# Six GELU evacuations ahead of the table sines, and two more weight strips on the ScalarE queue

## The chip, the cores and the metric

The kernel runs on one core of a Trainium2 chip. The metric is the device time of one execution in microseconds (us); lower is better. The core has five engines that run side by side: TensorE (PE in the profile, with PEld for its weight loads), VectorE (DVE), ScalarE (ACT), GpSimd (POOL) and SyncE (SP). They meet through semaphores; each takes its instructions in the order of the program. Loads and stores are put on queues by SyncE and ScalarE and carried by 16 DMA engines.

## What is computed

The input x has 2048 rows of 640 numbers in bfloat16. Two branches of it are mixed by a gate for each row:

```python
def _A_ref(x, Lambda_re, Lambda_im, B_re, B_im, C_re, C_im, log_dt, Dskip):
    Lam_bar = jnp.exp(jnp.exp(log_dt) * (Lambda_re + 1j * Lambda_im))
    B_bar = ((Lam_bar - 1.0) / Lam)[:, None] * Bmat
    Bu = jnp.einsum("bld,pd->blp", x + 0j, B_bar)
    for t in range(L):                       # 2048 steps
        h = Lam_bar[None, :] * h + Bu[:, t, :]
    y = 2.0 * jnp.einsum("blp,dp->bld", hseq, Cmat).real + x * Dskip
def _B_ref(x, w1, b1, w2, b2):
    h = _gelu(jnp.einsum("bsd,df->bsf", x, w1) + b1)     # 640 -> 1728, tanh form
    return jnp.einsum("bsf,fd->bsd", h, w2) + b2
g = sigmoid((x * gate_w).sum(-1, keepdims=True))
return g * a + (1 - g) * b
```

Branch A is a complex diagonal recurrence with 640 states, branch B a two-layer network with a GELU between.

## The kernel before

**Tiles and chunks.** The rows are worked in four chunks of 512. For each chunk c, TensorE multiplies by B (`ssm(c)`, matmuls at L536), by the first layer's weights (`ff1(c)`, L253), by the second layer's (`fin_b(c)`, L594 and L610) and by C (`fin_a(c)`, L653). All matmuls write to eight PSUM banks of 128x512 f32, which `bank()` hands out in turn; a bank is written again only after the engine that read it is done.

**First layer.** The 1728 hidden columns are 13 tiles of 128 (kf 0 to 12) and one of 64. The 640 input columns are 5 strips (kd 0 to 4) of weights. `w1a[kd]` holds the first FA = 6 tiles' weights of strip kd, `w1b[kd]` the rest, with one further column in which the gate's weight is put. `ff1_mm` does one matmul; `ff1_act` (L258) takes a full bank out through GELU with the bias `b1_c`, which lies in `colB`.

**The start.** For chunk 0, x is turned by TensorE itself (`turn`, L218, copies at L225 and L227) because it comes first. While the strips arrive, TensorE works kd by kd over six open banks (`strip(kd, ...)`): strips 0 and 2 by quarters of the chunk, then strip 1 whole, then strips 4 and 3 together, bank by bank. Parameters come as short rows in two tiles, `prmA` (log_dt and Lambda) and `prmB` (b1 and gate_w); one matmul with an identity turns each into columns (L329 to `colA`, L391 to `colB`). The matmul of prmB stands between kf 2 and kf 3 of strips 4 and 3. Five copies at L394 then put the gate's column into w1b.

**Tables.** The recurrence is made real by turning each state by its own angle, so cosines and sines of angle times row number are needed for 512 rows. VectorE makes the arguments for 128 rows (`u`, `kk`, `red`, `ab` at L370 to L380, and for a few special angles `two`, `kq`, `redq`, `absq` at L382 to L386). ScalarE takes four sines (L379, L381, L387, L388: `FS`, `FC`, `sq`, `cq`). VectorE extends them to 512 rows (L408 to L422: `TCOS`, `TSIN`). ScalarE computes sine, GELU and exponential from different function tables; a change is an ACT_TABLE_LOAD in the profile.

**The rest of VectorE's work.** For each chunk and each of five groups of states: products with the tables and a scan along the rows (`scan_ops`, L471 and L490). Then it puts x times D into banks (`seed`, L569) ahead of `fin_a`, and mixes the branches (L658). It scales C once (`fold(ks)`, five times): ScalarE makes two scaled copies `ft` (L453, L455; two buffers), VectorE adds them to C (L459). Folds 0 to 2 are put into `fin_b(0)`, folds 3 and 4 into `ff1(2)`, before kf 1 and kf 4. `gates(c)` (L551, L552) makes the gate's two factors from `gz`.

**Order.** Instructions of TensorE, VectorE and ScalarE stay in the order in which the program lists them. A small planner (`ck`, `later`, `let_out`) only chooses, when the program is built, after which group of matmuls a pending VectorE step is listed. The end of the program lists the stages:

```python
    ssm(0); gel_tile(1); ff1(1); gates(0)
    ssm(1, ...); gates(1)
    fin_b(0, {a: (lambda a=a: fold(a)) for a in range(3)})
    ff1(2, 0, {1: fold(3), 4: fold(4), 9: seed(0), 11: seed(1)})
    gates(2); fin_a(0); ssm(2); fin_b(1); fin_a(1); ssm(3); ff1(3)
    fin_b(2); gates(3); fin_a(2); fin_b(3); fin_a(3)
```

(Shortened: lambdas, tile allocations and the loads of x are left out.)

**Loads.** Before, two first strips (w1a 0 and 2) are issued by ScalarE; all other loads are issued by SyncE, in the order in which they stand, x first. There are eight semaphores for the completion of loads, used in turn; a load that reuses one waits on its queue until the earlier load with that semaphore has landed.

Of the kernel before, what the change touches and what calls it, by code (L numbers as in the profile page):

```python
# [11 lines left out]
ACT = mybir.ActivationFunctionType  # L12
# [4 lines left out]
P = 128  # L17
T = 2048
D = 640
F = 1728  # L20
CH = 512
NCH = T // CH
KD = D // P
# [12 lines left out]
TWO_PI_M = float(np.float32(2.0 * np.pi * (1.0 - 2.0 ** -20)))  # L36
# [5 lines left out]
def kernel(  # L42
# [19 lines left out]
    nc = tc.nc  # L62
# [12 lines left out]
    def bank(dtype=F32):  # L75
        return ps.tile([P, CH * 4 // (4 if dtype == F32 else 2)], dtype, name="bank")


    cut1 = FA * P
    n1b = F - cut1 + 1  # L80
    xT = [const.tile([P, KD, CH], BF16, name=f"xT{c}") for c in range(NCH)]
    w1a = [const.tile([P, cut1], BF16, name=f"w1a_{kd}") for kd in range(KD)]
    w1b = [const.tile([P, n1b], BF16, name=f"w1b_{kd}") for kd in range(KD)]
# [6 lines left out]
    ident = const.tile([P, P], BF16, name="ident")  # L90
    prmA = const.tile([P, P], BF16, name="prmA")
    NB = KS + KF - 1
    prmB = const.tile([P, P], BF16, name="prmB")
    colA = const.tile([P, 3 * KS], F32, name="colA")
    colB = const.tile([P, NB], F32, name="colB")
# [10 lines left out]
    halfpi = const.tile([P, 1], F32, name="halfpi")  # L106
# [8 lines left out]
    def load_xn(c, a0=0, a1=TPC, queue=None):  # L115
        if a0 == 0:
            xn[c] = xnp.tile([P, TPC, D], BF16, name="xn")
        r0 = c * CH + a0 * P
        (queue or nc.sync).dma_start(out=xn[c][:, a0:a1, :], in_=x2d[r0:r0 + (a1 - a0) * P, :].rearrange("(a p) d -> p a d", p=P))

    def load_w1a(queue, kd):
        queue.dma_start(out=w1a[kd][:], in_=B_w1[kd * P:(kd + 1) * P, 0:cut1])

    def rows(queue, dst, v):
        queue.dma_start(out=dst, in_=v.rearrange("(j p) -> j p", p=P))  # L125
# [2 lines left out]
    load_w1a(nc.scalar, 0)  # L128
    load_xn(0, 1, 2)
    load_w1a(nc.scalar, 2)  # L130
    warm = const.tile([P, 1], F32, name="warm")
    nc.scalar.activation(out=warm[:], in_=nc.const_aps.tensor(1.0, [P, 1], BF16), func=ACT.Exp)
    load_xn(0, 2, 3)
# [3 lines left out]
    rows(nc.sync, prmA[0:KS, :], A_log_dt)  # L137
    rows(nc.sync, prmA[KS:2 * KS, :], A_Lambda_im)
    rows(nc.sync, prmA[2 * KS:3 * KS, :], A_Lambda_re)
    for kd in (1, 4, 3):  # L140
        load_w1a(nc.sync, kd)
    rows(nc.sync, prmB[KS:NB, :], B_b1[0:(KF - 1) * P])
    rows(nc.sync, prmB[0:KS, :], gate_w)
    for kd in range(KD):
        nc.sync.dma_start(out=w1b[kd][:, 0:F - cut1], in_=B_w1[kd * P:(kd + 1) * P, cut1:F])  # L145
    make_identity(nc, ident[:])
    HC = CH // 4
    tfi = work.tile([P, HC], I32, name="e")
# [55 lines left out]
    def act(cost):  # L204
        ck.act = max(ck.act, ck.pe + 0.2) + cost
        return ck.act
# [6 lines left out]
    pA = bank()  # L213
# [25 lines left out]
    def col(name, dtype=F32, n=KS):  # L239
        return const.tile([P, n], dtype, name=name)  # L240
# [10 lines left out]
    def ff1_mm(p, c, kf, kd, t0=0, t1=CH, first=None, last=KD - 1):  # L251
        w = w1a[kd][:, kf * P:(kf + 1) * P] if kf < FA else w1b[kd][:, (kf - FA) * P:(kf - FA + 1) * P]
        nc.tensor.matmul(p[:, t0:t1], lhsT=w, rhs=xT[c][:, kd, t0:t1],  # L253
                         start=(kd == 0) if first is None else first, stop=(kd == last), skip_group_check=first is not None)
        pe(t1 - t0)

    def ff1_act(p, c, kf):
        nc.scalar.activation(out=gel[c][:, kf, :], in_=p[:, :], func=ACT.Gelu_apprx_tanh, bias=b1_c[:, kf:kf + 1])  # L258
        act(0.69)
# [51 lines left out]
    def strip(kd, t0, t1, first, f0=0, f1=FA):  # L311
        for kf in range(f0, f1):
            ff1_mm(banks[kf], 0, kf, kd, t0, t1, first, 3)
# [29 lines left out]
    strip(0, HT + P, CH, True)  # L343
    strip(2, HT + P, CH, False)
    strip(1, 0, CH, False)


    HB = 2 * HC

    def scratch(i):  # L350
        return scr[:, i * KS * HC:(i + 1) * KS * HC].rearrange("p (k i) -> p k i", k=KS)

    u, red, ab = scratch(0), scratch(1), scratch(2)
    m1, m2 = scratch(3), scratch(4)
    FSC = hsp.tile([P, 2 * KS, HB], F32, name="hs")
    FS = FSC[:, 0:KS, :]
    FC = FSC[:, KS:2 * KS, :]
# [3 lines left out]
    redq = col("redq", n=NQ * KS)  # L361
    absq = col("absq", n=NQ * KS)
    sq = col("sq", n=NQ * KS)
    cq = col("cq", n=NQ * KS)
# [11 lines left out]
    sQ, cQ = sq[:, 3 * KS:4 * KS], cq[:, 3 * KS:4 * KS]  # L376


    nc.scalar.activation(out=FS[:, :, 0:HC], in_=red, func=ACT.Sin, scale=TWO_PI_M)  # L379
    nc.vector.scalar_tensor_tensor(out=ab, in0=red, scalar=-1.0, in1=red, op0=ALU.mult, op1=ALU.max)  # L380
    nc.scalar.activation(out=FC[:, :, 0:HC], in_=ab, func=ACT.Sin, scale=-TWO_PI_M, bias=halfpi[:])  # L381
    nc.vector.tensor_tensor(out=two[:].rearrange("p (n k) -> p n k", n=NQ), in0=thp_c[:].rearrange("p (o k) -> p o k", o=1).to_broadcast([P, NQ, KS]),  # L382
                            in1=span4[:].rearrange("p (n o) -> p n o", o=1).to_broadcast([P, NQ, KS]), op=ALU.mult)
    nc.vector.tensor_copy(out=kq[:], in_=two[:])
    nc.vector.tensor_tensor(out=redq[:], in0=two[:], in1=kq[:], op=ALU.subtract)
    nc.vector.scalar_tensor_tensor(out=absq[:], in0=redq[:], scalar=-1.0, in1=redq[:], op0=ALU.mult, op1=ALU.max)  # L386
    nc.scalar.activation(out=sq[:], in_=redq[:], func=ACT.Sin, scale=TWO_PI_M)  # L387
    nc.scalar.activation(out=cq[:], in_=absq[:], func=ACT.Sin, scale=-TWO_PI_M, bias=halfpi[:])  # L388
    for kf in range(FA):
        if kf == 3:  # L390
            nc.tensor.matmul(pA[:, 0:NB], lhsT=prmB[:], rhs=ident[:, 0:NB], start=True, stop=True, skip_group_check=True)  # L391
            nc.vector.tensor_copy(out=colB[:], in_=pA[:, 0:NB])
            for j in range(KD):
                nc.vector.tensor_copy(out=w1b[j][:, n1b - 1:n1b], in_=pA[:, j:j + 1])  # L394
        for kd in (4, 3):
            ff1_mm(banks[kf], 0, kf, kd, 0, CH, False, 3)
    for kf in range(FA):
        ff1_act(banks[kf], 0, kf)
    two_banks = [bank(), bank()]
    for kd in range(KD):  # L400
        for i in range(2):
# [327 lines left out]
```

## Time and profile before

| what | us |
|---|---|
| three runs, device time | 216.41, 372.45, 215.88 (median 216.41) |
| the profiled execution, device time | 216.61 |
| its span in the profile | 214.7 |
| TensorE busy (matmuls) | 209.7 |
| VectorE busy | 190.2 |
| ScalarE busy | 101.4 |

The span runs from the first to the last instruction of the program; 1.9 us of the device time lie around it. A line of the timeline gives start, duration, engine, source line, operation, output<-inputs, shape and count, and in brackets the idle time before it with what ended it. A line of the waits gives who waited for whom, the total, the number of times and the longest. Names with q (SPq, ACTq) are the engines' sequencers, which issue loads.

### The profile page before, as it was taken

Reading aid. Unit: us, or ns where it says so; the run is one execution under the profiler, and the core shown is the slowest. Engines: PE = TensorE matmul, PEld = TensorE weight load, DVE = VectorE, ACT = ScalarE, POOL = GpSimd, SP = SyncE. Lnnn points to the kernel's source line nnn. Section 1 sums busy time; section 2 is a strip of 40 time slices with the busy share of each in tenths; the row PEclk is TensorE's granted clock in tenths of the full one; section 3 lists DMA queues with packets and bytes.
Section 4 is the critical chain, followed back from the end, with each engine's and each line's share of the span. In section 5 each row is a group of like instructions: output and inputs, shape, how many; then the busy total and the mean of one; then the engine's idle time right before and its main releaser. Section 6 shows DMA issues by size and latency. Waiting matters only on the chain.

```text
span 214.7 us, 3536 instructions
## 1 busy us (share of the span) xinstructions
PE 209.7 (98%) x1366; PEld 117.1 (55%) x1385; DVE 190.2 (89%) x396; ACT 101.4 (47%) x183; POOL 1.1 (0%) x12
## 2 busy tenths in 40 slices
PE   8999999999999999999999999999999999999994
PEld 4745444454455644775445577444454567654774
DVE  2899999999999999899999999999999999983153
ACT  3599556665875696302572310356683423204200
POOL 1000000000000000000000000000000000000000
PEclk9999999999999999999999999999999999999999
DMA  6899999993000000051000005100000000100011
GB/s 201 251 177 232 219 220 374 170 225 92 3 0 0 3 2 0 12 183 64 0 0 3 0 0 186 61 2 0 0 3 14 0 3 31 61 31 3 0 66 61
DMA packets 30419, 15.84 MB, mean 74 GB/s; under 512 B 22978, under 2 KB 30402, under 8 KB 30402
## 3 DMA queue, kind: packets, MB, share of 16 engines
q1 hardware_dynamic: 29970, 15.18, 29.3%
q10 hardware_dynamic: 432, 0.43, 0.6%
q8 instruction: 11, 0.18, 0.3%
q14 instruction: 6, 0.05, 0.1%
HBM read 7.48 MB, written 2.62 MB: 47 GB/s over the span
## 4 chain that ended last, share of the span: by engine, by line
PE 93%; DMA 3%; SPq 1%; issue 1%; DVE 0%
PE bank L594 26%; PE bank L253 23%; PE bank L653 20%; PE bank L536 20%; DMA w1b<-in_B_w_dram 3%; PE bank L215 1%; PE bank L610 1%; PE bank L279 1%; SPq L145 1%; PE bank L218 0%; SPq L125 0%; DVE ot L658 0%; DVE xT L225 0%; PE bank L269 0%
## 5 line engine op out<-in xcount | busy, mean ns | idle before, releaser
L594 PE MATMUL bank<-w_sb,gel 128*128 128x128 bf16 (+1 forms) x408 | 56.9, 297 | 0.7 <-issue 0.5
L594 PEld LDWEIGHTS <-gel 128*128 128x128 bf16 x416 | 32.2, 98 | 25.5
L539 ACT ACTIVATE bu<-bank 128x512 bf16<-128x512 f32 x40 | 23.9, 597 | 39.4 <-PE bank L536 39.3
L258 ACT ACTIVATE gel<-bank,colB 128x512 bf16<-128x512 f32 x52 | 34.1, 694 | 11.9 <-PE bank L253 11.1
L653 PEld LDWEIGHTS <-hs 128*128 128x128 bf16 x330 | 31.6, 98 | 11.5
L490 DVE TENSOR_TENSOR_SCAN g<-r_c,carry,v 128x512 bf16<-128x512 f32 x30 | 37.4, 1272 | 0.0
L602 ACT ACTIVATE gb<-bank,gcol 128x512 f32<-128x512 f32 (+1 forms) x32 | 15.1, 527 | 35.4 <-PE bank L610 19.3
L253 PE MATMUL bank<-xT,w1b 128*128 128x512 bf16 x137 | 31.0, 379 | 0.4 <-DMA w1b<-in_B_w_dram 0.2
L253 PE MATMUL bank<-xT,w1a 128*128 128x512 bf16 (+1 forms) x152 | 27.7, 334 | 0.2
L653 PE MATMUL bank<-CT_re,hs 128*128 128x320 bf16 (+2 forms) x165 | 27.1, 295 | 0.0
L653 PE MATMUL bank<-CT_im,hs 128*128 128x320 bf16 (+2 forms) x165 | 27.1, 295 | 0.0
L658 DVE SCALAR_TENSOR_TENSOR ot<-bank,gcol,gb 128x320 bf16<-128x320 f32 (+2 forms) x33 | 17.6, 535 | 9.2 <-PE bank L653 8.7
L536 PE MATMUL bank<-xT,BT_im 128*128 128x512 bf16 x99 | 24.8, 379 | 0.1
L536 PE MATMUL bank<-xT,BT_re 128*128 128x512 bf16 x97 | 24.4, 379 | 0.2
L253 PEld LDWEIGHTS <-w1b 128*128 128x128 bf16 x140 | 13.6, 98 | 16.9 <-DMA w1b<-in_B_w_dram 0.7
L253 PEld LDWEIGHTS <-w1a 128*128 128x128 bf16 x156 | 13.8, 101 | 12.5
L569 DVE TENSOR_TENSOR bank<-xn,Dbc 128x320 f32<-128x320 bf16 (+2 forms) x33 | 14.5, 483 | 3.5 <-ACT gb L602 3.4
L536 PEld LDWEIGHTS <-BT_im 128*128 128x128 bf16 x100 | 9.8, 98 | 11.8
L471 DVE TENSOR_TENSOR v<-wa,wb 128x512 bf16<-128x512 bf16 x40 | 15.2, 421 | 0.6
L536 PEld LDWEIGHTS <-BT_re 128*128 128x128 bf16 x100 | 9.6, 98 | 11.0
L583 ACT ACTIVATE bank<-b2bc 128x512 f32<-128x512 bf16 (+1 forms) x24 | 11.7, 529 | 6.2 <-DVE ot L658 6.2
L471 DVE TENSOR_TENSOR wa<-TCOS,g 128x1024 bf16<-128x1024 bf16 x20 | 13.7, 687 | 0.1
(100 smaller groups left out, 151.5 us busy)
## 6 DMA issues: line engine op xcount, KB each, us to landing
out_dram<-ot SPq DMA_DIRECT2D x15, 160.0 KB, 1.8
xn<-in_A_x_dram SPq DMA_DIRECT2D x6, 320.0 KB, 3.2
w_sb<-in_B_w_dram SPq DMA_DIRECT2D x3, 480.0 KB, 4.0
w1b<-in_B_w_dram SPq DMA_DIRECT2D x5, 240.0 KB, 6.1
xn<-in_A_x_dram SPq DMA_DIRECT2D x4, 160.0 KB, 3.1
w_sb<-in_B_w_dram SPq DMA_DIRECT2D x1, 640.0 KB
w1a<-in_B_w_dram SPq DMA_DIRECT2D x3, 192.0 KB, 2.9
w1a<-in_B_w_dram ACTq DMA_DIRECT2D x2, 192.0 KB, 3.6
```

Source lines behind the costliest of these rows:

```text
L253: nc.tensor.matmul(p[:, t0:t1], lhsT=w, rhs=xT[c][:, kd, t0:t1], start=(kd == 0) if first is None else first, stop=(kd == last), skip_grou ...
L258: nc.scalar.activation(out=gel[c][:, kf, :], in_=p[:, :], func=ACT.Gelu_apprx_tanh, bias=b1_c[:, kf:kf + 1])
L471: nc.vector.tensor_tensor(out=o, in0=a, in1=b, op=op)
L490: nc.vector.tensor_tensor_scan(s["g"][:, ri, :], r_c[:, ks:ks + 1].to_broadcast([P, CH]), s["v"][:, ri, :], init, ALU.mult, ALU.add)
L536: nc.tensor.matmul(p[:], lhsT=BT[ks >= KSA][:, kd, (ks % KSA if ks < KSA else ks - KSA) * P:][:, 0:P], rhs=xT[c][:, kd, :], start=(kd == 0 ...
L539: nc.scalar.activation(out=bu[:, ri, :], in_=p[:], func=ACT.Identity)
L569: dve_now(ck.pe, 0.45, lambda: nc.vector.tensor_tensor(out=p[:, 0:d1 - d0], in0=xn[c][:, a, d0:d1], in1=Dbc[:, d0:d1], op=ALU.mult))
L583: nc.scalar.activation(out=v, in_=src, func=ACT.Identity)
L594: nc.tensor.matmul(p[:, col:col + d1 - d0], lhsT=gel[c][:, kf, a * P:(a + 1) * P], rhs=w2_sb[:, kf, d0:d1], start=False, stop=False, skip_ ...
L602: nc.scalar.activation(out=gbs[ti][:, d0:d1], in_=p[:, col:col + d1 - d0], func=ACT.Identity, scale=gcol[:, 1, ti:ti + 1])
L653: nc.tensor.matmul(p[:, 0:d1 - d0], lhsT=hs[c][:, j, lo:lo + P], rhs=CT[:, j % KS, d0:d1], start=False, stop=(j == 2 * KS - 1), skip_group ...
L658: nc.vector.scalar_tensor_tensor(out=ot[:, d0:d1], in0=p[:, 0:d1 - d0], scalar=gcol[:, 0, ti:ti + 1], in1=gbs[ti][:, d0:d1], op0=ALU.mult, ...
```

## The change

Four things move; all other work is the same.

- The strips w1a 1 and w1a 4 are issued by ScalarE, after 0 and 2 and ahead of its warm-up activation. SyncE keeps only w1a 3.
- On SyncE the first part of w1b follows w1a 3, ahead of prmB's rows; the other four parts come after these.
- The matmul of prmB, the copy to colB and the five copies of the gate's column stand right behind strip 1 in the program, ahead of the table's arguments on VectorE and of strips 4 and 3 on TensorE.
- The six GELUs of kf 0 to 5 stand ahead of the four sines on ScalarE.

By the function tables, ScalarE's order is now exponential, GELU, sine, GELU.

```diff
     load_w1a(nc.scalar, 0)
     load_xn(0, 1, 2)
     load_w1a(nc.scalar, 2)
+    load_w1a(nc.scalar, 1)
+    load_w1a(nc.scalar, 4)
     warm = const.tile([P, 1], F32, name="warm")
...
-    for kd in (1, 4, 3):
-        load_w1a(nc.sync, kd)
+    load_w1a(nc.sync, 3)
+    def load_w1b(kd):
+        nc.sync.dma_start(out=w1b[kd][:, 0:F - cut1], in_=B_w1[kd * P:(kd + 1) * P, cut1:F])
+
+    load_w1b(0)
     rows(nc.sync, prmB[KS:NB, :], B_b1[0:(KF - 1) * P])
     rows(nc.sync, prmB[0:KS, :], gate_w)
-    for kd in range(KD):
-        nc.sync.dma_start(out=w1b[kd][:, 0:F - cut1], in_=B_w1[kd * P:(kd + 1) * P, cut1:F])
+    for kd in range(1, KD):
+        load_w1b(kd)
...
     strip(1, 0, CH, False)
+    nc.tensor.matmul(pA[:, 0:NB], lhsT=prmB[:], rhs=ident[:, 0:NB], start=True, stop=True, skip_group_check=True)
+    nc.vector.tensor_copy(out=colB[:], in_=pA[:, 0:NB])
+    for j in range(KD):
+        nc.vector.tensor_copy(out=w1b[j][:, n1b - 1:n1b], in_=pA[:, j:j + 1])
...
-    nc.scalar.activation(out=FS[:, :, 0:HC], in_=red, func=ACT.Sin, scale=TWO_PI_M)
     nc.vector.scalar_tensor_tensor(out=ab, in0=red, scalar=-1.0, in1=red, op0=ALU.mult, op1=ALU.max)
-    nc.scalar.activation(out=FC[:, :, 0:HC], in_=ab, func=ACT.Sin, scale=-TWO_PI_M, bias=halfpi[:])
...
-    nc.scalar.activation(out=sq[:], in_=redq[:], func=ACT.Sin, scale=TWO_PI_M)
-    nc.scalar.activation(out=cq[:], in_=absq[:], func=ACT.Sin, scale=-TWO_PI_M, bias=halfpi[:])
     for kf in range(FA):
-        if kf == 3:
-            nc.tensor.matmul(pA[:, 0:NB], lhsT=prmB[:], rhs=ident[:, 0:NB], start=True, stop=True, skip_group_check=True)
-            nc.vector.tensor_copy(out=colB[:], in_=pA[:, 0:NB])
-            for j in range(KD):
-                nc.vector.tensor_copy(out=w1b[j][:, n1b - 1:n1b], in_=pA[:, j:j + 1])
         for kd in (4, 3):
             ff1_mm(banks[kf], 0, kf, kd, 0, CH, False, 3)
     for kf in range(FA):
         ff1_act(banks[kf], 0, kf)
+    nc.scalar.activation(out=FS[:, :, 0:HC], in_=red, func=ACT.Sin, scale=TWO_PI_M)
+    nc.scalar.activation(out=FC[:, :, 0:HC], in_=ab, func=ACT.Sin, scale=-TWO_PI_M, bias=halfpi[:])
+    nc.scalar.activation(out=sq[:], in_=redq[:], func=ACT.Sin, scale=TWO_PI_M)
+    nc.scalar.activation(out=cq[:], in_=absq[:], func=ACT.Sin, scale=-TWO_PI_M, bias=halfpi[:])
```

## The prediction

> **What bounds the kernel now.** I read the page's busy shares first, then the chain that ended last, then who waited for whom.
>
> ```profile
> PE 209.7 (98%) x1366; PEld 117.1 (55%) x1385; DVE 190.2 (89%) x396; ACT 101.4 (47%) x183; POOL 1.1 (0%) x12
> PE 93%; DMA 3%; SPq 1%; issue 1%; DVE 0%
> PE bank L253 <- DMA w1b<-in_B_w_dram: 0.2, 1, 0.2
> ```
>
> TensorE is busy for 209.7 of 214.7 us and is 93% of the chain. It hardly ever stands still: after the start the waits name one stop, 0.2 us at 15.09, for the last load of w1b (0.39 us, counting the overlap of matmuls that is lost with it). So there is little to gain, and a delay elsewhere costs only if TensorE comes to wait for it. The engine to watch is VectorE, by its waits from 12 to 190 us:
>
> ```profile
> DVE gcol L551 <- ACT gz L285: 0.9, 1, 0.9
> DVE CT_re L459 <- ACT ft L455: 0.7, 2, 0.4
> DVE ot L658 <- DMA out_dram<-ot: 0.3, 1, 0.3
> ```
>
> In 178 us VectorE idles for 1.9 us, in four places. A delay put in at 13 us is thus carried almost whole through the kernel: VectorE has no idle time to make it up. The question is how late it may be before TensorE notices. The stage that the change rebuilds, on ScalarE's timeline:
>
> ```profile
> 8.66 1.28 ACT L379 ACT_TABLE_LOAD   x1
> 10.83 0.74 ACT L379 ACTIVATE hs<-gel 128x640 f32<-128x640 f32 x1 [0.88 <-DVE gel L372]
> 11.69 0.83 ACT L381 ACTIVATE hs<-gel,halfpi 128x640 f32<-128x640 f32 x1
> 12.42 0.20 ACT L387 ACTIVATE sq<-redq 128x20 f32<-128x20 f32 x1
> 12.53 0.30 ACT L388 ACTIVATE cq<-absq,halfpi 128x20 f32<-128x20 f32 x1
> 12.84 1.28 ACT L258 ACT_TABLE_LOAD   x1
> 14.14 7.79 ACT L258 ACTIVATE gel<-bank,colB 128x512 bf16<-128x512 f32 x13
> ```
>
> Columns: start, duration, instruction. The sines end at 12.83, and VectorE's first product with them (L408) starts at 12.86, directly behind its own earlier work. The 13 GELUs run back to back from 14.14, behind TensorE, but TensorE waits for none of them: kf 8's bank is wanted at 15.53 and its GELU has freed it at 14.83, and the later ones have 1.2 us or more.
>
> **What the Trainium skill says.** "ScalarE: Activation LUTs", section "What ACT_TABLE_LOAD costs", prices a change of function set at about 1283 ns of load plus 1380 ns of drain. The trace agrees with the first (1.28 us) and shows no drain: cq ends at 12.83, the load starts at 12.84, the GELU at 14.14. I use 1.30. "Table sets: the hidden batching unit" in the same page advises to batch by set; the change splits the GELUs around the sines, so three loads become four in the program's order. "DMA: Bandwidth & Descriptors", section "Issuing engines are not separate DMA queues", says that loads of ScalarE's and SyncE's queues run on the same 16 DMA engines and interleave. The trace agrees: from 1.75 to 4.3 us both queues moved about 0.39 MB each.
>
> **The change, part by part.**
>
> *Loads.* Two more 192 KB strips are issued on ScalarE's queue by about 2.5 us, beside SyncE's four 160 KB tiles of x. ScalarE's issue time is free: after its warm-up, done at 3.15 before, it waits until 4.44. In the old order the last x tile landed at 5.57 and the prmA rows at 5.80 (semaphore steps in the trace). With even sharing, when SyncE's 640 KB are through, ScalarE's queue has also moved 640 KB instead of 384: 256 KB more, at the page's 251 GB/s, 1.0 us. The last x tile then lands at 6.6, before its use at 7.68. The prmA rows queue behind it and also get new semaphore partners: their third load waits for the second x tile (4.48) instead of the first, so it is issued near 4.5 instead of 3.85. I put prmA at 6.8; TensorE wants it at 6.36. It stops there, so everything behind is x = 0.5 us late. Bounds: 0 (prmA's few rows are not held up) and 1.5 (the tiles of x and prmB, behind w1a 3 and w1b 0 now, come late too). The strips themselves land near 6 to 8, before their use from 9.28 on. w1b 1 to 4 wait for other partners and are issued about half a microsecond later; BT, next on SyncE, had over 4 us to spare (last BT landing 22.64, use 27.05).
>
> *prmB and the GELUs.* The prmB matmul now stands behind strip 1: 10.36 + 0.5 = 10.86. By the prmA pair (matmul 6.36, copy over at 6.76) colB is ready 0.40 later, 11.26. VectorE waits for it before it starts the table's arguments, which were made from 8.59 on under TensorE's strips: 3.79 us of work from u to absq, so done at about 15.5. The GELU needs both a bank and colB, and in the changed program the wait for colB stands ahead of the table load, so the load can't go early: 11.31, first GELU at 12.61. Six GELUs: 0.69 + 5 x 0.58 (four take 2.42) = 3.59, to 16.20; their banks are full by 13.7. Sine table: to 17.50, which hides the arguments' 15.5. First sine to second 0.64, from the second's start to cq's end 1.14 as before: 19.28. VectorE's table products thus start **D = 19.28 - 12.83 = 6.45 us** late. Another GELU table (1.30) follows, then seven GELUs to about 24.8; the first bank that TensorE wants from them is due at 21.65, freed near 21.3, the next ones with growing room. So no early stall there.
>
> *Where D reaches TensorE.* Nothing absorbs D up to the folds of C (L453, L455 on ScalarE, L459 on VectorE), where the two engines wait for each other through two buffers:
>
> ```profile
> 62.97 0.83 ACT L453 ACTIVATE ft<-CT_im,n2im 128x640 f32<-128x640 bf16 x1 [1.21 <-DVE CT_re L459]
> 76.19 0.89 DVE L459 SCALAR_TENSOR_TENSOR CT_re<-CT_re,c2re,ft 128x640 bf16<-128x640 bf16 x1 [0.38 <-ACT ft L455]
> 77.86 0.82 ACT L453 ACTIVATE ft<-CT_im,n2im 128x640 f32<-128x640 bf16 x1
> 78.58 0.82 ACT L455 ACTIVATE ft<-CT_re,n2im 128x640 f32<-128x640 bf16 x1
> 79.30 1.90 ACT L258 ACTIVATE gel<-bank,colB 128x512 bf16<-128x512 f32 x3
> ```
>
> The first line shows ScalarE already waiting for a fold; the later ft had 0.7 to 3.7 us of room, less than D. Behind the last ft (78.58) stand chunk 2's GELUs from kf 4 on. VectorE makes up 0.20 at 70.85 and 0.46 at 76.19, so fold 3 ends at 77.87 + 6.45 - 0.66 = 83.66; the ft behind it starts at 83.70 and ends at 84.52. GELUs of kf 4 to 8, overlapping by 0.10: first end 85.11, fifth 85.11 + 4 x 0.58 = 87.43 instead of 83.35. By the program's buffer order, kf 11's matmuls take the bank that kf 8's GELU frees; they start at 84.62 now and at 87.47 then: **+2.85 us** on TensorE, partly already at kf 10 (83.55, bank of kf 4).
>
> Second place, the seed of chunk 2 that TensorE needs soonest:
>
> ```profile
> 175.83 0.88 DVE L569 TENSOR_TENSOR bank<-xn,Dbc 128x320 f32<-128x320 bf16 x2
> 177.93 0.84 PE L653 MATMUL bank<-CT_re,hs 128*128 128x320 bf16 x5
> ```
>
> The first of these two seeds ends at 176.31, 1.62 before its matmul, and starts right behind a scan, so it shifts with VectorE. By then VectorE has also made up 0.96 at gcol and 0.41 at 97.34: 6.45 - 0.66 - 0.96 - 0.41 = 4.42 late, seed at 180.73, matmul at 177.93 + 2.85 = 180.78. No further stall; but this second place alone would also ask for 2.8. At the end fin_a of chunk 3 has over 4 us of room.
>
> *Sum.* The early 0.5 us and the w1b wait (0.39 back) lie inside the 2.85, because TensorE waits at 84.6 for VectorE's clock and not its own. The end moves by D - 3.60. Against the profiled execution: 216.61 + 2.85 = 219.5. The median shown is 216.41, 0.2 lower, so the forecast is **219.3 us**, 1.3% slower. A comparison of this kernel tells about 2% from no change.
>
> **Rivals.**
> 1. *Not slower*: VectorE's lateness never reaches TensorE, and the loads only fill the w1b gap. This decides if D stays under 3.6. For it: 98% on TensorE, and most waits had over 4 us of room. Against: six GELUs and two table loads alone are 6 us. Time: 216.4 - 0.4 + 0.4 (prmA) = 216.4, or 216.0 with x at 0.
> 2. *The GELU table is loaded at 8.7 after all*, during the wait for colB: D = 5.2, end +1.6, 218.0. Against: the place of the wait in the program's order.
> 3. *Early bandwidth*: the four strips starve x, prmA and prmB. Each microsecond of x adds one to D and so to the end; from x = 2.0 on it passes 2%: D = 7.95, +4.35, 220.8; with x = 2.5, 221.3. For it: the DMA row is full here. Against: only 256 KB are put ahead.
>
> **How the numbers follow.** Forecast 0.65, its own range 218.4 to 220.5 (x from 0 to 1.5, with 0.3 for ScalarE's spacing); rival 1 0.10, rival 2 0.10, rival 3 0.15. The range 217.2 to 221.2 leaves out rival 1 and the far half of rival 3. No case is 2% faster: 0.01. Over 2% slower: rival 3 and the edge of the forecast, 0.16. The rest, 0.83, is within 2%.
>
> **What would show it.** In the profile after: four table loads; first GELU near 12.6, cq's end near 19.3, L408 directly after it with VectorE idle some 4 us before; TensorE waiting for a GELU (L258) at L253 between 83 and 88 us for 2 to 3 us in all; a stop at prmA's matmul of about 0.5. No TensorE wait there, or VectorE idle times of several microseconds between 60 and 100 us that swallow D, would make it wrong; so would prmA or prmB landing over 1.5 us late.

## The result and the profile after

Four executions of the changed kernel took 223.73, 221.37, 224.37 and 221.95 us, median **222.84 us**, against 216.42 for the kernel before on the same chip. The ratio is 1.031 with a 95% interval of 1.020 to 1.041: slower, where 219.3 had been forecast with a range up to 221.2. The profiled execution is the one of 223.73 us, with a span of 221.8 (before 216.61 and 214.7). The granted clock of TensorE, averaged over an execution, was 0.985, 1.0, 0.992 and 0.992 in the four, in this order. It goes with the spread of 3 us only in part: the slowest execution is not the one with the lowest clock. One execution of the kernel before took 372.45 us, for which no trace gives a reason; the ratio leaves it out.

Line numbers are 4 or 5 higher than in the kernel before: L253 is now L258, L258 is L263, L329 is L334, L408 is L412, L453, L455 and L459 are L457, L459 and L463. L391, the matmul of prmB, is L351.

From the page, the busy shares, the chain's shares and the granted clock in 40 slices:

```profile
PE 213.7 (96%) x1385; PEld 118.6 (53%) x1385; DVE 190.3 (86%) x396; ACT 101.4 (46%) x184; POOL 1.1 (0%) x12
PE 61%; DVE 28%; ACT 6%; DMA 3%; issue 1%; SPq 0%; ACTq 0%
PEclk9799999999999999699999999999999999999999
```

TensorE's share of the chain fell from 93 to 61%. VectorE, which had none, has 28%, ScalarE 6%. ScalarE has one instruction more, the fourth table load. TensorE is busy for 4 us more; part of that is 19 more matmuls in the records, and the clock row shows another part: two slices have a lower digit, one at the start and one near 90 us.

The waits, of which four lines carry the reading (who waited for whom, total us, times, longest):

```profile
DVE gel L412 <- ACT cq L402: 4.0, 1, 4.0
DVE colB L352 <- PE bank L351: 2.4, 1, 2.4
PE bank L258 <- ACT gel L263: 2.5, 2, 1.4
PE bank L334 <- DMA prmA<-in_A_Lambda_re_dram: 2.1, 1, 2.1
```

TensorE stops once for the prmA rows, 2.1 us, and twice for a GELU, 2.5 us together. VectorE stands idle for 4.0 us ahead of its first table product. The stop for w1b is gone. The start, from the timeline:

```profile
8.21 0.17 PE L334 MATMUL bank<-ident,prmA 128*128 128x15 bf16 x1 [2.09 <-DMA prmA<-in_A_Lambda_re_dram]
13.35 0.17 PE L351 MATMUL bank<-ident,prmB 128*128 128x18 bf16 x1
13.84 1.28 ACT L263 ACT_TABLE_LOAD   x1 [2.57 <-DVE colB L352]
15.14 3.58 ACT L263 ACTIVATE gel<-bank,colB 128x512 bf16<-128x512 f32 x6
18.73 1.28 ACT L399 ACT_TABLE_LOAD   x1
21.50 0.30 ACT L402 ACTIVATE cq<-absq,halfpi 128x20 f32<-128x20 f32 x1
21.83 0.82 DVE L412 TENSOR_TENSOR gel<-hs,cq 128x640 f32<-128x640 f32 x1 [4.03 <-ACT cq L402]
```

The sines end at 21.80; before it was 12.83. So D, VectorE's lateness, is 8.97 us. And where it reaches TensorE, from the chain in order of time (start, us, what):

```profile
84.55 0.81 DVE CT_re L463
85.38 0.84 ACT ft L457
86.24 0.83 ACT ft L459
87.06 2.90 ACT gel L263 x5
90.00 4.00 PE bank L258 x10
```

A fold on VectorE, two scaled copies on ScalarE, five GELUs, then kf 11's matmuls: the chain that the prediction had drawn, link by link. The matmuls start at 90.00 instead of 84.62, and ten of them take 4.00 us. In the kernel before they stand in a row of 22 without a stop, and these ten took 2.32 us (84.62 to 86.94):

```profile
81.82 5.13 PE L253 MATMUL bank<-xT,w1b 128*128 128x512 bf16 x22
```

For the clock, the busy times in two pairs of stretches of 3.41 us. The columns are the stretch, its length, busy us (and instructions) of PE, PEld, DVE, ACT and POOL, then the granted clock, the DMA share and GB/s:

```profile
4.77:8.18 3.41, 1.36 (x22) 1.12 (x20) 0.62 (x2) 0.54 (x2) 0.00 (x0) 1.00 0.86 281
8.18:11.59 3.41, 3.38 (x33) 3.40 (x34) 1.91 (x9) 1.07 (x4) 0.00 (x0) 0.50 0.75 231
86.69:90.10 3.41, 1.34 (x6) 0.58 (x6) 3.41 (x5) 3.41 (x7) 0.00 (x0) 1.00 0.01 2
90.10:93.51 3.41, 3.41 (x9) 1.22 (x9) 3.41 (x8) 1.98 (x4) 0.00 (x0) 0.50 0.00 0
```

Twice a stretch in which TensorE was busy for only 1.35 us is followed by one at half clock. So each stop was paid twice on the spot: as a wait, and as slow matmuls right after it. What is left of the second payment at the end of the kernel is another matter, taken up below.

### The profile page after: what moved, and what is told of

Same layout as the page of the kernel before. It is cut to its first block, busy times and chain, and to the rows that moved or that the text cites. A ratio compares the mean times of both kernels' runs of the same rounds, so it can differ in the third digit from the quotient of the medians.

```text
span 221.8 us, 3557 instructions
## 1 busy us (share of the span) xinstructions
PE 213.7 (96%) x1385; PEld 118.6 (53%) x1385; DVE 190.3 (86%) x396; ACT 101.4 (46%) x184; POOL 1.1 (0%) x12
## 4 chain that ended last, share of the span: by engine, by line
PE 61%; DVE 28%; ACT 6%; DMA 3%; issue 1%; SPq 0%; ACTq 0%
PE bank L657 20%; PE bank L598 19%; PE bank L258 10%; PE bank L540 10%; DVE g L494 6%; DVE wb L475 4%; DVE wa L475 4%; ACT gel L263 3%; DVE v L475 2%; DVE hs L475 2%; DMA prmA<-in_A_Lambda_re_dram 2%; DVE CT_re L463 1%; DMA w1a<-in_B_w_dram 1%; DVE g L425 1%; DVE TSIN L426 1%; DVE TCOS L426 1%
## 5 line engine op out<-in xcount | busy, mean ns | idle before, releaser
L598 PE MATMUL bank<-w_sb,gel 128*128 128x512 bf16 (+1 forms) x416 | 57.9, 299 | 0.0
L263 ACT ACTIVATE gel<-bank,colB 128x512 bf16<-128x512 f32 x52 | 33.6, 691 | 11.3 <-PE bank L258 11.2
L657 PEld LDWEIGHTS <-hs 128*128 128x128 bf16 x330 | 31.6, 98 | 11.5
L258 PE MATMUL bank<-xT,w1b 128*128 128x512 bf16 x140 | 33.0, 394 | 2.5 <-ACT gel L263 2.5
L258 PE MATMUL bank<-xT,w1a 128*128 128x512 bf16 (+1 forms) x156 | 28.7, 343 | 0.0
L657 PE MATMUL bank<-CT_re,hs 128*128 128x320 bf16 (+2 forms) x165 | 27.1, 295 | 0.0
L657 PE MATMUL bank<-CT_im,hs 128*128 128x320 bf16 (+2 forms) x165 | 27.1, 295 | 0.0
L258 PEld LDWEIGHTS <-w1b 128*128 128x128 bf16 x140 | 14.1, 101 | 20.5 <-issue 5.2
L258 PEld LDWEIGHTS <-w1a 128*128 128x128 bf16 x156 | 14.6, 105 | 12.3
```

What stands on the lines that cost most here:

```text
L598: nc.tensor.matmul(p[:, col:col + d1 - d0], lhsT=gel[c][:, kf, a * P:(a + 1) * P], rhs=w2_sb[:, kf, d0:d1], start=False, stop=False, skip_ ...
L657: nc.tensor.matmul(p[:, 0:d1 - d0], lhsT=hs[c][:, j, lo:lo + P], rhs=CT[:, j % KS, d0:d1], start=False, stop=(j == 2 * KS - 1), skip_group ...
```

## The experiments

The theory to be tested: D reaches TensorE at kf 10 and 11 as D - 3.60; what was missed is a late prmA and the half clock. The rivals: VectorE's lateness costs elsewhere too; the loads alone do it; the four table loads are harmless and only the number of GELUs ahead counts.

| kernel | median us | ratio to before, 95% interval |
|---|---|---|
| the change | 222.84 | 1.0306 (1.0204 to 1.0408) |
| e_order: the new order alone | 220.79 | 1.0233 (1.0199 to 1.0266) |
| e_loads: the new loads alone | 217.30 | 1.0063 (1.0044 to 1.0082) |
| e_order3: three GELUs ahead of the sines | 219.48 | 1.0160 (1.0138 to 1.0182) |
| e_order0: no GELU ahead of the sines | 218.37 | 1.0118 (1.0083 to 1.0153) |
| e_order_xn: e_order, chunk 2's x loaded later | 219.41 | 1.0147 (1.0119 to 1.0175) |
| e_order_ft: e_order, four buffers for ft | 220.37 | 1.0187 (1.0163 to 1.0211) |
| e_after_prmA: the change, prmA's rows early | 223.61 | 1.0355 (1.0321 to 1.0390) |
| e_after_warm: the change, idle TensorE kept busy | 221.15 | 1.0223 (1.0207 to 1.0239) |
| e_loads1: one strip moved instead of two | 216.57 | 1.0034 (1.0017 to 1.0051) |
| e_best: the last part of w1b by ScalarE | 217.86 | 1.0085 (1.0070 to 1.0100) |
| e_best2: the same, later | 218.16 | 1.0111 (1.0069 to 1.0154) |
| e_order_fetch: e_order, TensorE's program made longer ahead | 219.94 | 1.0160 (1.0136 to 1.0184) |

The kernel before lay between 215.95 and 216.42 beside them.

### The two halves apart

**e_order** has the two moves of order with the loads as before (the diff shows part of it):

```diff
     strip(1, 0, CH, False)
+    nc.tensor.matmul(pA[:, 0:NB], lhsT=prmB[:], rhs=ident[:, 0:NB], ...)
+    nc.vector.tensor_copy(out=colB[:], in_=pA[:, 0:NB])
...
     for kf in range(FA):
         ff1_act(banks[kf], 0, kf)
+    nc.scalar.activation(out=FS[:, :, 0:HC], in_=red, func=ACT.Sin, scale=TWO_PI_M)
...
```

> The change without its loads: prmB's matmul behind strip 1 and six GELUs ahead of the sines, all loads as before. Theory (the end moves by D - 3.60, D being how late VectorE's first table product is): no stop at prmA, first GELU near 12.1, cq's end near 18.8, D = 6.0, the matmuls of kf 11 in chunk 2 2.4 us late, 218.8 us; if the two stops before them make TensorE's clock fall to half for the next 3.4 us, up to 220.6. Rival (the loads do all the harm, the new order is hidden): 216.4.

Its sines end at 18.69, D = 5.87: the prediction's own 5.95 (6.45 less its 0.5 for x) within 0.1. kf 11 should then start 2.27 late, at 86.89. TensorE's stops from the timeline (in brackets the idle time and what ended it):

```profile
84.60 1.24 PE L253 MATMUL bank<-xT,w1b 128*128 128x512 bf16 x4 [1.40 <-ACT gel L258]
86.91 2.32 PE L253 MATMUL bank<-xT,w1b 128*128 128x512 bf16 x10 [1.07 <-ACT gel L258]
178.95 0.84 PE L652 MATMUL bank<-CT_re,hs 128*128 128x320 bf16 x5 [1.05 <-DVE bank L568]
182.32 0.84 PE L652 MATMUL bank<-CT_re,hs 128*128 128x320 bf16 x5 [0.50 <-DVE bank L568]
```

kf 11 starts at 86.91, and with no drop of the clock its ten matmuls take 2.32 us again. But two further stops stand at the seeds of chunk 2, the prediction's "second place": the matmul of 177.93 starts at 182.32, 4.39 late, where the prediction's sum gives 2.27. The time is 2.0 us above the expected 218.8, and the clock had no part in it. VectorE did not make up 0.41 us near 97; it lost time there, in a wait of its own:

```profile
102.86 0.55 DVE L657 SCALAR_TENSOR_TENSOR ot<-bank,gcol,gb 128x320 bf16<-128x320 f32 x1 [1.65 <-PE bank L535]
```

The profile names a matmul of ssm as what ended this wait, but that matmul has no part in it. In the profile of the change the same instruction waits 1.34 us and is said to wait for the store, out_dram<-ot. `ot` has two buffers, so L657 waits for the store of two tiles before. I took the store for the cause and tested that in two ways.

**e_order_xn** is e_order with the two loads of x for chunk 2 (320 KB each), which stand on SyncE just ahead of that store, issued by ScalarE after ssm(2):

```diff
     fin_a(0)
-    load_xn(2, 0, H)
-    load_xn(2, H, TPC)
     ssm(2, {KS - 1: lambda: first_banks(1)})
+    load_xn(2, 0, H, nc.scalar)
+    load_xn(2, H, TPC, nc.scalar)
```

> e_order, but the two loads that refill x's tile for chunk 2 are issued by ScalarE after the ssm of chunk 2, and no longer by SyncE between the first two output stores. Theory: in e_order the second store stands behind these 640 KB, and VectorE waits 1.65 us at 102.9 for it, since the output has two buffers; that is what makes it late for the seeds of chunk 2 (TensorE's stops of 1.05 and 0.50 us at 179 and 182). Without the loads in front the wait and both stops go: 219.2, 1.5 less than e_order. Rival (VectorE's lateness comes from the start alone): 220.8 as e_order.

The wait on VectorE and both stops at the seeds are gone, the two at kf 10 and 11 are unchanged (1.41 and 1.07), and the time fell from 220.79 to 219.41. So the wait is for the store, which goes behind the loads of x. In e_order the store was issued at 97.94 and its last part landed at 102.77, 4.8 us later; in the kernel before it took 3.5 us (93.73 to 97.25), and without the loads ahead of it 1.9 us (97.92 to 99.79). In the profiled execution of this kernel (220.31 us; the others took 218.94 to 219.43) the clock dropped once:

```profile
83.08:86.49 3.41, 1.35 (x5) 0.48 (x5) 3.41 (x7) 3.38 (x7) 0.00 (x0) 1.00 0.01 2
86.49:89.90 3.41, 2.94 (x8) 1.01 (x7) 3.41 (x8) 2.47 (x5) 0.00 (x0) 0.50 0.00 0
```

It is the same pattern as in the change, a stretch with 1.35 us busy and then half clock. The same two stops had cost no clock in e_order. Its clock records start at 5.782, and counted from there in steps of 3.413 us the two stops fell into two stretches:

```profile
80.88:84.29 3.41, 2.32 (x11) 0.97 (x10) 3.41 (x6) 1.98 (x3) 0.00 (x0) 1.00 0.00 0
84.29:87.70 3.41, 1.98 (x8) 0.87 (x9) 3.41 (x5) 3.41 (x7) 0.00 (x0) 1.00 0.01 2
```

So the same stops are followed by half clock in one execution and not in another. The drop hides no stop here: the seed was ready at 180.13, and at full clock TensorE would have come for it at about 180.3.

**e_order_fetch** asks why the same store behind the same loads takes longer in e_order than before. In e_order's trace 15 of its 16 parts had landed by 101.69, and the last came 1.1 us later. A fetch of instructions, one packet of 16 KB, was under way at 98.45 for 1.42 us, early in the burst of loads and store; in the kernel before it came at 96.53, at the end of the burst. The guess is that both want the same DMA engine, which the packet records do not name. If the place of the fetch depends on how far a program has been read, a longer program for TensorE ahead of everything should move it, with no change in the work:

```diff
-    for n in (512, 512, 512, 512, 512, 512, 128, 128):
+    for n in (128,) * 26:
         nc.tensor.matmul(pA[:, 0:n], lhsT=ones(P), rhs=ones(n), start=True, stop=True)
```

> e_order with the warm-up of TensorE cut into 26 matmuls of 128 columns instead of 8 of 512 or 128 (3328 columns in both). All work that counts is the same, but TensorE's program is 18 matmuls and as many weight loads longer ahead of everything else. Theory: VectorE's wait for the store of ot near 102.9 us in e_order (1.65 us, against 0.33 in the kernel before) comes from a 16 KB fetch of instructions that shares one DMA engine with the loads of x and the store: the trace shows such a fetch at 98.45 for 1.42 us in e_order, inside the burst from 97 to 102.8, and in the kernel before at 96.53, at the burst's end. With 24 matmuls added to the change, the fetch came 6.5 us earlier against the burst. So here it comes near 93 to 94, ahead of the burst; the wait falls to about 0.3 us, the stops at chunk 2's seeds from 1.55 to at most 0.5, and the time from 220.8 to 219.2 to 219.7 us. Rival: the store is late because it stands behind 640 KB of loads, wherever the fetch falls: wait 1.3 to 1.7, seeds' stops 1.5, 220.8 us.

```profile
101.54 0.55 DVE L657 SCALAR_TENSOR_TENSOR ot<-bank,gcol,gb 128x320 bf16<-128x320 f32 x1 [0.37 <-DMA out_dram<-ot]
```

The fetch came at 95.94 and was over at 97.04, before the burst. All parts of the store landed by 101.45, 3.4 us after its issue at 98.03, and the wait is 0.37 us instead of 1.65: the store behind the loads is not late in itself. The median is 0.85 us lower than that of e_order, less than the 1.1 to 1.6 expected. No stop at the seeds shows, but in the profiled execution the ten matmuls behind kf 11's stop ran at half clock (3.99 us), which made TensorE itself late enough to hide one. An estimate from its times: the seed ended at 180.94 and its matmul started at 181.83; 1.67 us of clock less would have brought TensorE there at 180.16, so about 0.8 us would have been lost, where e_order lost 2.1 (4.39 late there, 2.29 at kf 11). So moving the fetch took away the larger part, not all.

The other profiles line up with this. Counted from the issue of the first load of x, the fetch came after 1.0 to 1.6 us in four kernels (waits 1.51 to 2.11), after 3.2 to 3.3 in two, the change among them (1.34 and 1.25), after 3.7 to 4.0 in five, the kernel before among them (0.33 to 0.61), and ahead of it in two (0.30 and 0.37). That the two share one DMA engine is not shown.

**e_loads** has the loads of the change and the order of before (the diff is the first two parts of the change).

> Only the change's loads: w1a 1 and 4 by ScalarE, w1b 0 ahead of prmB's rows; prmB's matmul and the GELUs where they were. Theory: prmA lands near 8.1, TensorE stops 2.1 us for it and then runs at half its clock to about 11.6 (0.85 us more), gets 0.4 back at w1b: 2.5 us late from its own side. The sines are late by about 2.9, under 3.6, so VectorE adds nothing: 218.9. Rival (early lateness of TensorE is harmless, or the stop comes only with the new order): 216.4.

217.30, less than expected.

```profile
7.29 0.17 PE L334 MATMUL bank<-ident,prmA 128*128 128x15 bf16 x1 [1.13 <-DMA prmA<-in_A_Lambda_re_dram]
```

The prmA rows land at 7.16, the stop is 1.13 us and not 2.1, the clock holds at 1.0, and VectorE's delay (0.93) stays under 3.6, so the stop for prmA is all it costs; w1b's 0.39 us come back. With the order alone at 4.6 us and the loads alone at 1.1, the sum is 5.7 of the 6.4 measured.

### How many GELUs ahead

**e_order3** and **e_order0** are e_order with the first three, or none, of the six GELUs ahead of the sines:

```diff
-    for kf in range(FA):
+    for kf in range(3):
         ff1_act(banks[kf], 0, kf)
     nc.scalar.activation(out=FS[:, :, 0:HC], in_=red, func=ACT.Sin, scale=TWO_PI_M)
...
+    for kf in range(3, FA):
+        ff1_act(banks[kf], 0, kf)
```

> As e_order, but only three GELUs (kf 0 to 2) ahead of the sines, the other three behind them; the same four table loads. Theory: three GELUs less, 3 x 0.58 = 1.74, so D = 4.25 and the end 0.65 later than before: 217.1, with no clock fall. Rival (no threshold, the loss goes with the lateness): two thirds of the loss of e_order or more, so 218.0 or above.

> As e_order, but the four sines ahead of all GELUs again: of the new order only prmB's matmul and the colB copies stay early, and there are three table loads. Theory: VectorE waits for colB before it makes the table's arguments, D = 2.7, under 3.6, so nothing reaches TensorE: 216.4. Rival (every lateness of VectorE is passed on): 219.

D came out at 4.11 (4.25 expected) and 2.54 (2.7 expected), and the stops at kf 10 and 11 are gone in both. The fourth table load is not harmless: in e_order3 the third GELU ends at 13.86 and the first sine starts at 15.17, with nothing but the load of 1.28 us between. Yet both took about 2 us more than expected. In e_order3 the wait for the store of `ot` is 1.79 us and the seeds stop TensorE for 1.36 and 0.50; besides, TensorE stops for banks of the later GELUs, 0.59 us at 18.99 and 0.29 at 19.57. In e_order0 the sines themselves are late, since the copies of prmB now stand ahead of their arguments, and all GELUs behind them:

```profile
17.42 3.40 PE L253 MATMUL bank<-xT,w1b 128*128 128x512 bf16 x15 [1.19 <-ACT gel L258]
```

So ScalarE has two customers at the start, the banks and the tables, and each order of the two makes one of them late. Before, the sines stood first and their arguments were ready at 10.83: both were in time.

### The second buffer of the folds

**e_order_ft** is e_order with four buffers for the scaled copies, in bfloat16, so that ScalarE need not wait for a fold:

```diff
-        t1 = fwork.tile([P, D], F32, name="ft", bufs=2)
-        t2 = fwork.tile([P, D], F32, name="ft", bufs=2)
+        t1 = fwork.tile([P, D], BF16, name="ft", bufs=4)
+        t2 = fwork.tile([P, D], BF16, name="ft", bufs=4)
```

> e_order with four buffers for the scaled copies ft instead of two (in bfloat16, to keep the room), so that ScalarE no longer waits in the folds for VectorE. Theory: the two stops of TensorE at kf 10 and 11 (2.5 us) go, but VectorE is as late as ever, and the stops move to the seeds of fin_a, where TensorE then waits for about 3.5 us in all: 219.9 to 220.8. Rival (the fold is the only place where lateness counts): 218.3.

The stops at kf 10 and 11 are gone, and 2.5 us less of waiting there bought 0.4 us: TensorE now stops at seeds instead, 0.69 us at 88.09, 1.16 at 126.29, 1.17 at 178.89 and 0.50 at 182.26. VectorE's lateness reaches TensorE at the next place where they meet. This is the clearest sign that the lateness, and not a place, is the cause.

### prmA, bandwidth and the clock

**e_after_prmA** is the change with prmA's three row loads issued right behind the first tile of x (the diff shows their new place; they leave the old one).

```diff
     load_w1a(nc.scalar, 0)
+    rows(nc.sync, prmA[0:KS, :], A_log_dt)
+    rows(nc.sync, prmA[KS:2 * KS, :], A_Lambda_im)
+    rows(nc.sync, prmA[2 * KS:3 * KS, :], A_Lambda_re)
     load_xn(0, 1, 2)
```

> The whole change, but with prmA's three rows issued by SyncE right after the first x tile. Theory: no stop at prmA and no clock fall there, so D is 6 again and the end is that of e_order, less the w1b stop of 0.4 where that lies on the path: 220.4 to 220.8. Rival (the strips on ScalarE's queue also hold up x or prmB): 222 and above.

From the waits of SyncE and from the timeline:

```profile
SPq L119 <- DMA w1a<-in_B_w_dram: 1.5, 1, 1.5
6.43 0.45 PE L223 MATMUL bank<-ident,xn 128*128 128x128 bf16 x5 [1.66 <-DMA xn<-in_A_x_dram]
```

The stop at prmA is gone, but the second tile of x lands at 6.38 instead of 4.5 and TensorE stops for it for 1.66 us ahead of 6.43. The three rows take three of the eight semaphores, so SyncE, with the second tile next, waits 1.5 us until a strip has landed, and issues it at 3.69 instead of 1.19. The median is 223.61 where 220.4 to 220.8 was expected: nothing was gained.

**e_after_warm** is the change with 24 matmuls of ones ahead of prmA's matmul, into a corner of the bank that nothing reads, to keep TensorE busy while it waits:

```diff
     strip(0, P, HT, True)
+    for _ in range(24):
+        nc.tensor.matmul(pA[:, CH - 192:CH], lhsT=ones(P), rhs=ones(192), ...)
     nc.tensor.matmul(pA[:, HT:HT + 3 * KS], lhsT=prmA[:], ...)
```

> The whole change, with 24 matmuls of ones (192 columns, 1.9 us, in an unused part of pA) put ahead of prmA's matmul, to keep TensorE busy while it waits. Theory: the stop takes as long as before, but the clock doesn't fall behind it; the strips up to 12 us run at full pace and D is 0.85 smaller where the clock fell before. Median 222, and a narrower spread than the 221.4 to 224.4 of the change. Rival (the slow matmuls at 8 to 11.6 us come from their operands, not from the idle time before): 222.8, with the same slow stretch.

The rows land as late as in the change (8.04 and 8.08), but 1.7 us of the median are back (0.8 had been expected) and all four executions lie within 0.4 us at clock 1.0. From its timeline:

```profile
8.17 0.17 PE L336 MATMUL bank<-ident,prmA 128*128 128x15 bf16 x1 [0.39 <-DMA prmA<-in_A_Lambda_re_dram]
12.17 0.17 PE L353 MATMUL bank<-ident,prmB 128*128 128x18 bf16 x1
```

From prmA's matmul to prmB's it is 4.00 us, as in the kernel before (6.36, and 10.36 for the end of strip 1). In the change it is 5.14 (8.21 to 13.35). So the half clock in the start costs 1.14 us, and useless matmuls are enough to avert it. D is then 7.79, kf 11 starts at 88.83: D - 3.60 = 4.19, measured 4.21. The two stops at kf 10 and 11 are there (1.40 and 1.08) and no drop followed them.

**e_loads1** moves one strip, w1a 1, to ScalarE's queue instead of two, in the order of before.

```diff
     load_w1a(nc.scalar, 2)
+    load_w1a(nc.scalar, 1)
...
-    for kd in (1, 4, 3):
+    for kd in (4, 3):
```

> The kernel before with only w1a 1 moved to ScalarE's queue (192 KB beside x instead of 384). Theory (prmA's rows stand behind x on SyncE's queue and get only half of the engines while ScalarE's queue has strips): prmA lands at about 6.6, between the 5.8 of before and the 7.2 to 8.1 seen with two strips; TensorE stops for 0.3 us or so and has it back at w1b; 216.3, within 0.3 of before. Rival (what matters is which earlier load's semaphore the rows wait for): the third row's load waits for an x tile or strip that lands before 4, as before, so no stop at all.

```profile
6.71 0.17 PE L330 MATMUL bank<-ident,prmA 128*128 128x15 bf16 x1 [0.58 <-DMA prmA<-in_A_Lambda_re_dram]
```

prmA's last row lands at 6.62, against 5.80 with no strip moved and 7.16 with two (e_loads). The first strip of 192 KB delays the rows by 0.82 us, the second by another 0.54. The rival was the semaphore for which the rows' loads wait, and their issue does get later, from 3.85 to 4.18 and 4.82. But the last tile of x, issued at 2.12 each time, lands at 5.57, 6.43 and 7.09, and the rows 0.23, 0.19 and 0.07 us behind it: they come when x is through, so it is the shared transfer that delays them. The median is 216.57, 0.6 above the kernel before at its side, where 0.3 had been expected at most.

In the profile of the change the rows landed at 8.08, with the same loads as e_loads. There four of the five packets of the last row had landed by 7.28 and the fifth came at 8.08, and the other two rows look the same; it was so in e_after_warm too, and not in e_loads. Why one packet lags in one kernel and not in the other was not found.

### The one gain the change has, alone

**e_best** and **e_best2** try to take the 0.39 us of w1b's stop without the rest: the last of w1b's five parts goes to ScalarE's queue, behind its first copy of x (e_best) or behind its last (e_best2).

```diff
-    for kd in range(KD):
+    for kd in range(KD - 1):
         nc.sync.dma_start(out=w1b[kd][:, 0:F - cut1], ...)
...
     nc.scalar.activation(out=r_c[:], in_=dtl[:], func=ACT.Exp)
+    nc.scalar.dma_start(out=w1b[KD - 1][:, 0:F - cut1], ...)
```

> A try for a version faster than both: the kernel before, with the last part of w1b issued by ScalarE behind its copy of the second x tile (near 6.1 us) instead of last on SyncE's queue. Theory: it lands by 12 instead of 15.04, TensorE's stop of 0.39 us goes, nothing else is late since the strips behind it have over 1.4 us of room; VectorE is as late as before and still early enough: 0.4 us less, 0.2%. Rival (it takes bandwidth from w1a 1, prmB or the w1b parts, and the stop comes there): no gain.

> The kernel before with one edit: the last of the five strips of w1b is issued by ScalarE, behind its activation for r_c, that is after its last copy of x, instead of by SyncE. Theory: ScalarE is free there until VectorE delivers the first sine argument, so the issue and its wait for a free queue place hold up nothing that TensorE needs; the strip lands by about 14 us instead of 15.04, the stop of 0.39 us that TensorE makes for it in the kernel before goes, and the time falls by about 0.2 to 0.4 us, to 0.998 to 0.999 of before. Rival: the issue blocks ScalarE past 10.83 us, where its first table load starts in the kernel before; then the sines and GELUs come later by as much, banks are late, and the time is up by 0.5 us or more.

In e_best the part landed at 13.8 and TensorE no longer stopped for it. But ScalarE could not issue the load before 8.63, since its semaphore was still held by a load of prmB, and behind it stood a copy of x:

```profile
9.03 0.21 ACT L332 ACTIVATE dt<-colA 128x5 bf16<-128x5 f32 x1 [3.28 <-DMA prmB<-in_B_b_dram]
9.56 0.27 PE L218 MATMUL bank<-ident,xn 128*128 128x128 bf16 x2 [1.93 <-ACT xT L227]
```

In e_best2 the issue of the load ends at 10.1, about 1.6 us later than that of SyncE's last w1b load in the kernel before (8.53), and the load lands at 16.58 instead of 15.04: TensorE stops 1.39 us for it. Here the theory of a gain and its rival both failed: no GELU became late (D = 0.39) and yet the time rose. No kernel of this study is faster than the one before.

## Why the prediction was wrong, step by step

- **Loads, x = 0.5: the step that failed.** Measured by the matmul of prmB, 13.35 against 10.36, x is 2.99, twice the upper bound of 1.5. With this x alone the forecast would have been 219.3 + 2.5 = 221.8. It has two parts. prmA's matmul is 1.85 late: even sharing put the last tile of x at 6.6 and the rows at 6.8. They landed at 7.09 and 7.16 with the same loads in e_loads, where two strips took 1.36 us and not 1.0, and at 8.08 in the change, where one packet of each row came later still. The further 1.14 us are the half clock after the stop, of which no step took account. That prmA came 2.28 us late was among the prediction's own signs of being wrong. Rival 3 had this mechanism: "each microsecond of x adds one to D and so to the end".
- **prmB and the GELUs: right.** colB to the first GELU, the six GELUs (3.58, forecast 3.59), the table loads (1.28 and nothing behind) and the sines give D = 5.98 + x in the change, against 5.95 + x in the sum. Everything from 11.26 on is late by 2.5, the error of x. Rival 2, the early table load, did not happen: the load at 13.84 waits for colB.
- **Where D reaches TensorE first: right.** kf 11 is 5.38 late, D - 3.60 = 5.37. In e_order it is 2.29 for 2.27, in e_after_warm 4.21 for 4.19, and in e_order_xn, e_after_prmA and e_order_fetch, where D is 5.91, 7.11 and 5.83, it is 2.34, 3.53 and 2.24. The forecast of a wait of 2 to 3 us in all for GELUs held (1.39 and 1.07); it lies from 86.3 to 90.0 rather than between 83 and 88.
- **The clock after these stops: not in the sum.** Ten matmuls took 4.00 us instead of 2.32: 1.68 us. With 1.35 more of the wait at prmA and 1.14 of the first drop, it makes 4.17; on the 219.5 that the prediction gave for the profiled execution, 223.7. It took 223.73. This is an account of that one execution. The others had one drop or none by their mean clock and took 221.37 (none), 221.95 and 224.37 (one each); what else made them differ is in no trace.
- **"VectorE makes up 0.41 at 97.34": wrong, and hidden in the change.** The wait is for a store, which VectorE's own earlier work sets off, so its landing moves along and it is no slack. In e_order it grew to 1.65 us, with an instruction fetch in the burst of its loads and store, and the second place, which the prediction put level with the first, stopped TensorE for another 1.55. In the change the wait was 1.34 us, and no stop shows:

```profile
184.36 0.88 DVE L573 TENSOR_TENSOR bank<-xn,Dbc 128x320 f32<-128x320 bf16 x2
184.99 0.84 PE L657 MATMUL bank<-CT_re,hs 128*128 128x320 bf16 x5
```

  The first of these two seeds ended at 184.83, and its matmul, 7.06 late, started at 184.99. Without the 1.68 us of the second drop TensorE would have come at 183.31 and waited for the seed for about 1.6 us, by an estimate from these times. So the two failures overlap: of the second drop only about 0.1 us is left at the end of the kernel, and a sum with the clock put right would still have missed this place.
- **Rival 1, lateness that never arrives: wrong.** It took D under 3.6 to keep kf 11 in time; e_order0 shows that such an order costs elsewhere.
- **w1b's stop: right**, it is gone and bought nothing.

Part by part, the order alone costs 4.6 us of the 6.4, the loads alone 1.1. The rest, 0.7, appears only with both; a prmB that is late by the loads then delays the GELUs too, and a clock drop at the start stands in no profile but that of the change. It was not split further, and it is smaller than the interval of the change's own ratio (1.020 to 1.041, or 4.4 to 8.8 us), so it may be noise.

## What to carry to other kernels

When an engine with hardly any idle time is made late at the start, look for each place where the bound engine meets it and subtract that place's slack; removing one such place only hands the lateness to the next. Before counting a wait as time to be made up, see whether what ends it is a transfer that moves along. A price read at one place is not yet a price at the end, when a second place would have asked for the same time. A load moved to another queue takes its bandwidth from the loads that the first instructions need, and a load on a compute engine's queue can hold up that engine until a semaphore is free.

## What the runs showed of the hardware

- **A stop of TensorE is followed by half clock, now and then.** The Trainium skill, "TensorE: Matmul & The Clock Gate", section "Part 1: The HAM clock gate (the "warmup" mystery)", says that the clock is halved by a monitor with free-running windows of 3413 ns. The clock records agree: 8.179 to 11.592 and 90.099 to 93.512 are 3.413 us each. The page ties the half clock to an idle window of about 3.4 us. Here the window ahead of it was not idle: in the change TensorE was busy for 1.34 and 1.36 of its 3.41 us, in e_order_xn for 1.36, in e_order_fetch for 1.24. In no profile with clock records, its windows counted on from the first record, did half clock follow a window with 1.75 us busy (the start of e_after_prmA) or more, and no window within a kernel lay between. Two stops of 1.4 and 1.1 us were enough when they fell into one window, and cost nothing when a window ended between them, as in e_order. On the spot the price was 1.14 and 1.68 us.
- **Loads of 1.2 KB landed only when the large loads ahead of them on the queue were through.** The last row of prmA landed 1.95 us after issue before (3.85 to 5.80) and 3.4 us after it in the change (4.69 to 8.08). In e_loads1 and e_loads it landed at 6.62 and 7.16, within 0.2 us of the last tile of x.
- **A store lands later when an instruction fetch falls into its burst.** One packet of 16 KB took 0.9 to 2.1 us, and the store took 4.8 us to land in e_order, with its last part 1.1 us behind the others, against 3.4 us in e_order_fetch, with the fetch ahead of the burst. With 18 matmuls more at the start the fetch came at 95.94 instead of 98.45, so an edit elsewhere can move it. How the one delays the other is not shown.
